# One TensorE semaphore increment per unit and bank, in a spectral and feed-forward kernel on one core

## The chip, the core and the metric

The kernel runs on one core of a Trainium2 chip. The core has a matmul engine (TensorE; PE in the profile, with its weight loads listed apart as PEld), VectorE (DVE), ScalarE (ACT), GpSimd (POOL), a queue engine that issues most transfers (SyncE; SP), and 16 DMA engines. Each engine runs its own list of instructions in order. They wait for each other through semaphores: an instruction can add to a counter when it is done, and an instruction of another engine can wait until that counter has reached a number.

The metric is the device time of one execution in microseconds (us). For the kernel before it is 258.02 us, the median of three runs (257.98 to 258.78).

## The reference

Four steps follow each other on a matrix of 2048 rows (S) by 448 columns (D), in bf16. Two of them (A) are a two-dimensional Fourier filter of the normalised input, two (B) are a feed-forward layer with a squared ReLU. Both A steps use the same filter, both B steps the same weights.

```python
def _A_ref(x, w_r, w_i):
    X = rfft2(x.astype(float32))              # over rows and columns
    y = irfft2(X * (w_r + 1j * w_i), s=(S, D)).astype(bfloat16)
    return y
def _B_ref(x, w1, b1, w2, b2):
    h = einsum("bsd,df->bsf", x, w1) + b1     # 448 -> 1792
    h = where(h > 0, h, 0); h = h * h
    return einsum("bsf,fd->bsd", h, w2) + b2  # 1792 -> 448
x = A_x
x = x + _A_ref(_layernorm(x), A_w_r, A_w_i)
x = x + _B_ref(_layernorm(x), B_w1, B_b1, B_w2, B_b2)
x = x + _A_ref(_layernorm(x), A_w_r, A_w_i)
x = x + _B_ref(_layernorm(x), B_w1, B_b1, B_w2, B_b2)
```

## The kernel before

The Fourier transforms are matmuls with constant matrices, in stages. Stage A1 (first layer) or A2 (second) transforms part of the rows into `XA`; stage TD transforms the columns, into `U` (the buffer is `arena`); stage B goes on with the rows, into `EF` (also `arena`); stage W multiplies by the filter on VectorE, into `T3` (the buffer is `wide`); stage Bi is the first half of the way back along the rows, into `VT`; stages TI and AI undo the rest, into `wide` and `x_sb`. The feed-forward layer follows: normalised rows are transposed by DMA (L708) or by matmuls with `J_sb` into `wide`, `h_part` and `h_pairs` make the hidden layer in `arena`, and `o_tile` multiplies it by the second weights and adds to `x_sb`. In the first feed-forward layer, `fold` and two additions per tile of rows (L775, `wide<-xin`) and `second_A` already begin the second Fourier layer.

All results of matmuls go to PSUM, a memory of eight banks. ScalarE or VectorE copies them out (L746 on ACT, L747 on DVE, both from `evac`); then the bank can be used again.

The kernel is written through a recorder. Each operation is added to `_Sched` with what it reads and writes, and `add` finds the operations that it depends on (`op.deps`): the last writer of what it reads, and the last writer and all the readers of what it overwrites. So an operation on VectorE that overwrites a buffer read by sixteen matmuls depends on all sixteen. Matmuls are gathered in units, runs of matmuls that are issued one behind the other; a matmul knows the PSUM tile that it adds to (`d.tile`), and a copy knows the tiles that it takes out (`op.takes`). The order of the units on each engine is written out by hand in `ORDER`.

`schedule` ends with a loop that marks each operation that anybody depends on (`has_dep`). `assign_tickets` numbers the marked operations of an engine 1, 2, 3 and so on. `emit` writes the instructions out: a marked operation increments its engine's semaphore by one when it is done, and an operation that depends on others waits for the highest of their numbers on each engine, unless its engine has waited for as high a number already. A dependency between two matmuls needs no wait, except in `h_pairs`, where matmuls on the two halves of the array add to one tile and one half waits for the other.

Stage Bi matters below. One of its units has 32 matmuls: two streams of 16, one on the upper and one on the lower 64 rows of the array, interleaved so that two matmuls run beside each other. Its stationary operand is a piece of `T3` (`wide`), its moving operand a piece of `H_sb` (128 columns). Each layer has eight such units:

```python
u = sch.new_unit("pe", 64, "row")
m = _Tile(2) if v in MERGE else None
...
if m:
    evac(V.rearrange("p t q c -> p q t c"), m[...], EV["Bi"])
else:
    for q in range(2):
        evac(V[:, :, q], t[q][...], EV["Bi"])
```

For the five units v in `MERGE` one copy takes both streams (1,024 columns); for the other three there are two copies of 512 columns, and each waits for the last matmul of its stream. The unit issued last, in either layer, is of the second kind. Stage TI begins when all eight units have been copied to `VT`. In the gaps of its plan the kernel issues matmuls on a tile of ones (L1361), whose results nobody uses. All other matmuls are recorded by one helper, `mm`, and bear its line, L721.

Of the kernel before, what the change touches and what calls it, by code (L numbers as in the profile page):

```python
# [291 lines left out]
class _Sched:  # L292
# [83 lines left out]
    def schedule(self):  # L376
# [100 lines left out]
        while total:  # L477
# [26 lines left out]
            start, u, e = choice[0][0], choice[1], choice[2]  # L504
            if e == "pe":

                while self.warm_fn is not None:
# [15 lines left out]
                    d = _Op("pe", self.warm_fn(bk[1], n), False, unit, 195.0)  # L523
# [56 lines left out]
        self.done = done  # L580
        for e in self.ENGINES:
            for op in self.ops[e]:
                for d in op.deps:
                    d.has_dep = True

# [867 lines left out]
```

## Time and profile before

| | before |
|---|---|
| median of three runs | 258.02 us |
| the profiled execution | 258.13 us |
| its span, first to last instruction | 256.3 us |
| PE busy | 247.0 us, 2,462 matmuls |
| DVE busy | 193.3 us |
| ACT busy | 167.2 us |
| granted TensorE clock | 1.00 throughout |
| matmuls of stage Bi (`ps<-H_sb,wide`) | 512, in 29.1 to 38.3 us and 147.0 to 156.5 us |

Times in views of the trace count from the first instruction of the program. In a timeline row stand the start, the length from the first to the last of the instructions taken together, the engine, the line, the operation, the buffers (`out<-in`), the shapes, the number of instructions, and in square brackets the idle time of the engine just before and who ended it. "issue" stands where the profile shows nothing that was waited for. The chain of work that ended last goes from the last instruction back, at each step to what released it; its rows give start, length, engine, buffer and line.

### The profile page before, as it was taken

The numbers are of one execution on the slowest core, as the hardware profiler recorded it, in microseconds if no ns is written. First come the engines' busy times: TensorE is split into PE (matmuls) and PEld (weight loads), VectorE is DVE, ScalarE is ACT, GpSimd is POOL, SyncE is SP. The second block draws the span as 40 slices with busy tenths as digits, with TensorE's granted clock in tenths as the row PEclk, the third lists the DMA queues.
The fourth block names the chain that finished last, engine by engine and source line by source line (L and its number), as shares of the span: only waits on it lengthen the run. The fifth ranks groups of instructions, "written<-read, shape, count | busy, mean of one in ns | idle before, by whom it ended". The sixth has DMA issues, their size and how long they took to land.

```text
span 256.3 us, 6151 instructions
## 1 busy us (share of the span) xinstructions
PE 247.0 (96%) x2462; PEld 154.4 (60%) x2462; DVE 193.3 (75%) x628; ACT 167.2 (65%) x362; POOL 12.5 (5%) x26
## 2 busy tenths in 40 slices
PE   7899988999999999999999998999999999999996
PEld 2578677886544555554567677898544445544454
DVE  3994988889872899997999997999993079320543
ACT  5896988995287894016847997999459784006600
POOL 3870000000000000000000000000000000000000
PEclk9999999999999999999999999999999999999999
DMA  6999944121111000130000000021134001152004
GB/s 196 372 329 372 290 142 145 33 48 36 48 41 43 0 4 0 41 42 3 0 3 1 3 3 3 3 41 45 42 79 41 0 3 24 39 92 72 3 0 145
DMA packets 24080, 18.10 MB, mean 71 GB/s; under 512 B 16082, under 2 KB 22706, under 8 KB 24052
## 3 DMA queue, kind: packets, MB, share of 16 engines
q1 hardware_dynamic: 22756, 13.22, 19.8%
q0 software_dynamic: 576, 3.69, 4.1%
q10 hardware_dynamic: 720, 0.80, 0.9%
q8 instruction: 19, 0.31, 0.5%
q14 instruction: 9, 0.07, 0.1%
HBM read 12.20 MB, written 1.84 MB: 55 GB/s over the span
## 4 chain that ended last, share of the span: by engine, by line
PE 82%; DMA 7%; ACT 4%; DVE 3%; issue 1%; POOL 1%; SPq 0%; DVEq 0%; POOLq 0%
PE ps L721 81%; DMA Wt<-in_A_w_r_dram,ix 4%; ACT arena L746 2%; DMA FA_sb<-c_FA 2%; DMA wide<-wide 2%; ACT wide L746 1%; DVE wide L775 1%; ACT VT L746 1%; DVE x_sb L1214 1%; PE ps L1361 0%; POOL Wt L824 0%; DVE arena L747 0%; POOL Fs L758 0%; DVE st L851 0%; SPq L713 0%
## 5 line engine op out<-in xcount | busy, mean ns | idle before, releaser
L721 PE MATMUL ps<-wide,W_sb 64*128 64x512 bf16 (+1 forms) x770 | 90.0, 346 | 0.1
L721 PE MATMUL ps<-W_sb,arena 128*128 128x448 bf16 (+3 forms) x476 | 86.8, 342 | 0.0
L721 PEld LDWEIGHTS ps<-wide,W_sb 64*128 64x128 bf16 (+1 forms) x770 | 51.4, 95 | 36.1 <-DMA wide<-wide 0.9
L740 ACT ACTIVATE arena<-ps,b1col 128x512 bf16<-128x512 f32 x84 | 51.9, 691 | 29.1 <-PE ps L721 28.8
L721 PEld LDWEIGHTS ps<-W_sb,arena 128*128 128x128 bf16 x476 | 45.6, 98 | 38.1 <-ACT arena L740 0.4
L775 DVE TENSOR_TENSOR arena<-arena 128x512 bf16<-128x512 bf16 (+1 forms) x140 | 44.0, 362 | 29.7 <-ACT arena L740 29.7
L1092 ACT ACTIVATE VT<-x_sb 128x448 bf16<-128x448 bf16 x28 | 16.1, 582 | 13.2 <-DVE x_sb L1068 13.2
L746 ACT ACTIVATE arena<-ps 128x896 bf16<-128x896 f32 (+1 forms) x27 | 20.6, 839 | 3.3 <-PE ps L721 3.3
L740 ACT ACTIVATE mv<-mv,epst 128x1 f32<-128x1 f32 (+1 forms) x45 | 12.8, 297 | 11.9 <-DVE mv L852 11.6
L775 DVE TENSOR_TENSOR wide<-arena,Wt 128x896 bf16<-128x896 bf16 x32 | 17.7, 619 | 1.2 <-DMA Wt<-in_A_w_r_dram,ix 1.2
L740 ACT ACTIVATE arena<-ps 128x256 bf16<-128x256 f32 x56 | 17.9, 400 | 0.9 <-PE ps L721 0.7
L746 ACT ACTIVATE XA<-ps 128x512 bf16<-128x512 f32 (+1 forms) x28 | 15.3, 596 | 3.3 <-PE ps L721 3.3
L721 PE MATMUL ps<-H_sb,wide 64*128 64x128 bf16 x512 | 16.0, 216 | 0.9 <-issue 0.6
L1214 DVE SCALAR_TENSOR_TENSOR x_sb<-ps,mv,xin 128x448 bf16<-128x448 f32 (+2 forms) x13 | 8.0, 643 | 11.7 <-PE ps L721 11.5
L721 PEld LDWEIGHTS ps<-H_sb,wide 64*128 64x128 bf16 x512 | 14.4, 94 | 3.3 <-issue 1.6
L721 PE MATMUL ps<-wide,VT 64*128 64x512 bf16 x42 | 15.8, 376 | 0.0
L746 ACT ACTIVATE wide<-ps 128x896 bf16<-128x896 f32 (+3 forms) x20 | 14.1, 762 | 2.2 <-DVE wide L747 1.1
L746 ACT ACTIVATE VT<-ps 128x512 bf16<-128x512 f32 (+1 forms) x16 | 12.6, 822 | 1.7 <-PE ps L721 1.4
L1361 PE MATMUL ps<-ones 128*128 128x512 bf16 (+2 forms) x32 | 10.1, 437 | 2.8 <-ACT VT L746 1.1
L757 ACT ACTIVATE wide<-x_sb,rstd 128x448 bf16<-128x448 bf16 x12 | 7.8, 665 | 6.3 <-DVE mv L784 6.0
L747 DVE CAST arena<-ps 128x448 bf16<-128x448 f32 (+1 forms) x11 | 8.8, 831 | 3.2 <-PE ps L721 3.2
L1068 DVE SCALAR_TENSOR_TENSOR x_sb<-ps,mv,xin 128x448 bf16<-128x448 f32 x16 | 10.3, 676 | 0.8 <-PE ps L721 0.7
(79 smaller groups left out, 274.7 us busy)
## 6 DMA issues: line engine op xcount, KB each, us to landing
out_dram<-x_sb SPq DMA_DIRECT2D x15, 112.0 KB, 1.8
W_sb<-in_B_w_dram SPq DMA_DIRECT2D x1, 1568.0 KB, 7.8
H_sb<-c_H SPq DMA_DIRECT2D x2, 768.0 KB, 10.9
W_sb<-in_B_w_dram SPq DMA_DIRECT2D x1, 1344.0 KB, 11.7
xin<-in_A_x_dram SPq DMA_DIRECT2D x3, 224.0 KB, 4.8
G_sb<-c_G SPq DMA_DIRECT2D x1, 512.0 KB, 6.0
xin<-in_A_x_dram ACTq DMA_DIRECT2D x2, 224.0 KB, 4.6
VT<-in_B_w_dram SPq DMA_DIRECT2D x2, 192.0 KB, 3.2
```

The source lines that it names most:

```text
L721: return sch.add("pe", lambda e: e.matmul(_res(o), lhsT, rhs, start=start, stop=stop, skip_group_check=skip), [lhsT, rhs], [o], cost=cost, ...
L740: sch.add("act", lambda e: e.activation(o, _res(i), func, **kw), rd, [o], cost=c)
L746: op = sch.add(engs[0], lambda e: e.activation(o, _res(i), ACT.Copy) if h[0].eng == "act" else e.tensor_copy(o, _res(i)), [i], [o], cost=c ...
L747: e.tensor_copy(o, _res(i)), [i], [o], cost=c[engs[0]], unit=unit)
L757: op = sch.add(engs[0], lambda e: e.activation(o, i, ACT.Copy, scale=s) if h[0].eng == "act" else e.tensor_scalar(o, i, s, 1.0, op0=ALU.mu ...
L775: sch.add(eng, lambda e: e.tensor_tensor(o, _res(a), b, op), [a, b], [o], cost=_free(o) / rate + 69.0)
L1068: small(lambda e, xx=xx, xi=xi, r=r, m=m: e.scalar_tensor_tensor(out=xx, in0=_res(r), scalar=m, in1=xi, op0=ALU.subtract, op1=ALU.add), [r ...
L1092: op = sch.add("act", lambda e, i=i, o=o, x=x, h=h: e.activation(o, x, ACT.Square, accum_out=sd[:, i, 1:2]) if h[0].eng == "act" else e.sc ...
L1214: small(lambda e: e.scalar_tensor_tensor(out=o, in0=_res(i), scalar=rs[0] if rs else 1.0, in1=xi, op0=ALU.add if t >= 4 and last else ALU. ...
L1361: return lambda e: e.matmul(ps[:, b, 0:n], ones[:], ones[:, None, :].to_broadcast([P, n // P, P]), start=True, stop=True)
```

## The change

Three lines are added to the loop at the end of `schedule`:

```diff
         for e in self.ENGINES:
             for op in self.ops[e]:
+                if e != "pe":
+                    op.deps = [d.unit.ops[-1] if d.eng == "pe" and d.unit is not None and d.tile not in op.takes else d
+                               for d in op.deps]
                 for d in op.deps:
                     d.has_dep = True
```

An operation of another engine that depends on a matmul because it overwrites what the matmul reads now depends on the last matmul of that matmul's unit instead. An operation that copies the matmul's tile out of PSUM keeps its dependency on the last matmul of that tile. So matmuls in the middle of a unit are no longer marked, unless a tile ends with them or another half of the array waits for them, and only marked ones increment the semaphore. In the built programs 1,937 of the 2,462 matmuls increment the semaphore before, and 401 after; of the 512 matmuls of stage Bi all 512 before, and 22 after.

The order of instructions on every engine stays as it is, and so do their operands. The numbers that others wait for change, since there are fewer marked matmuls. Ten waits name another matmul than before: two on DVE (L775, `wide<-xin`), eight on SP (six transposes and two transfers into `VT`); two of the eight fall away, since SP has waited for as much already. All lines behind the change have numbers higher by three.

## Prediction

> **What bounds the kernel now.** I read the page first: the shares of busy time, then the chain that ended last, by engine.
>
> ```profile
> span 256.3 us, 6151 instructions
> PE 247.0 (96%) x2462; PEld 154.4 (60%) x2462; DVE 193.3 (75%) x628; ACT 167.2 (65%) x362; POOL 12.5 (5%) x26
> PE 82%; DMA 7%; ACT 4%; DVE 3%; issue 1%; POOL 1%; SPq 0%; DVEq 0%; POOLq 0%
> ```
>
> TensorE carries the chain for 82% of the span. An edit that changes no matmul can gain in two ways: the matmuls come closer together, or one of the short stretches shrinks in which the chain leaves PE. The chain in order of time shows where those are (start, length, who):
>
> ```profile
> 33.40 0.38 issue
> 33.78 3.75 PE ps L721 x127
> ...
> 37.78 0.99 PE ps L721 x13
> 38.77 0.69 DVE VT L747
> 39.46 0.14 issue
> 39.60 5.66 PE ps L721 x74
> ...
> 45.29 90.69 PE ps L721 x699
> ...
> 153.60 3.59 PE ps L721 x96
> 157.19 0.59 ACT VT L746
> ...
> 157.83 0.39 PE ps L1361
> ...
> 163.66 58.14 PE ps L721 x461
> ...
> 253.99 0.03 issue
> 254.01 0.33 DVE x_sb L1214
> ```
>
> Two things are to be seen. From 45.29 to 135.98 and from 163.66 to 221.80 PE runs without leaving the chain, so whatever comes earlier ahead of these stretches ends the kernel earlier by as much. And the chain leaves PE behind stage Bi of both layers: at 38.77 for a copy into `VT` on DVE, at 157.19 for one on ACT. TI cannot start before these copies.
>
> **Do the increments slow the matmuls?** Stage Bi is the densest place. Two stretches of its matmuls alone (length; busy and count of PE, then of PEld; clock, DMA), and their group on the page (busy us, mean ns):
>
> ```profile
> 33.78:37.31 3.53, 3.53 (x127) 3.53 (x128) 1.00 0.48 111
> 153.60:156.46 2.86, 2.86 (x96) 2.68 (x96) 1.00 0.02 6
> ...
> L721 PE MATMUL ps<-H_sb,wide 64*128 64x128 bf16 x512 | 16.0, 216 | 0.9 <-issue 0.6
> ```
>
> 3.53 us by 126 steps is 28.0 ns a matmul. In the second row the last matmul's own 0.216 us (the mean in the group's row) comes off: 2.64 by 95 is 27.8 ns. At the full clock and without a gap, all of these matmuls increment the semaphore. So increments do not hold PE back, and I cost the matmuls' own pace at **nothing gained**.
>
> **Do they delay those who wait?** These are the copies of stage Bi in the first layer, and the end of its matmuls:
>
> ```profile
> 34.42 1.02 ACT L746 ACTIVATE VT<-ps 128x1024 bf16<-128x1024 f32 x1
> 35.51 0.60 ACT L746 ACTIVATE VT<-ps 128x512 bf16<-128x512 f32 x1
> 36.01 1.02 ACT L746 ACTIVATE VT<-ps 128x1024 bf16<-128x1024 f32 x1
> 37.70 1.02 ACT L746 ACTIVATE VT<-ps 128x1024 bf16<-128x1024 f32 x1 [0.68 <-PE ps L721]
> 37.78 0.55 PE L721 MATMUL ps<-H_sb,wide 64*128 64x128 bf16 x13 [0.25 <-issue]
> 38.76 0.69 DVE L747 CAST VT<-ps 128x512 bf16<-128x512 f32 x1 [0.92 <-PE ps L721]
> ```
>
> The copies at 34.42, 35.51 and 37.70 belong to the units issued fourth, fifth and seventh, and each waits for the last matmul of its unit. One unit (32 increments) lies between the first two, two (64) between the latter: 1.09/32 = 34.1 ns and 2.19/64 = 34.2 ns. PE issues a matmul every 28.0 ns, so the copies keep step with something slower than the matmuls, and fall behind by 32 x 6.1 = 0.2 us a unit. The lag is there to be seen: PE's last matmul ends at 37.78 + 0.55 = 38.33, while the copies start at 38.76. For a plain distance take the last two rows of the chain: from the end of the last matmul to the addition it is 0.03. So I read the semaphore as taking one increment of TensorE every 34 ns, with a queue behind it that empties only where PE pauses.
>
> The Trainium skill, "TensorE: Matmul & The Clock Gate", section "The cost: per-tile semaphore tail", says that increments on every matmul serialise and states 26.3 ns for each in the tail. The serialising agrees with the rows above; the figure doesn't, since 26.3 is less than the 28.0 ns between matmuls, and by it no queue would form here and the sum below would be nil.
>
> **The sum, first layer.** Of a unit's 32 increments one or two stay, so nothing queues. The last copy on DVE then starts at 38.33 + 0.03, about 38.36 instead of 38.76. That is 0.40 us earlier; its matmul is the last but one, which ends some 0.03 before 38.33, so I take **0.42**. The copy on ACT beside it goes as early, because the one ahead of it (37.70) waited 0.68 itself. Earlier in the layer another wait shrinks:
>
> ```profile
> 31.53 1.09 ACT L746 ACTIVATE VT<-ps 128x512 bf16<-128x512 f32 x2 [0.34 <-PE ps L721]
> 32.66 0.39 PEld L721 LDWEIGHTS ps<-H_sb,wide 64*128 64x128 bf16 x14 [0.23 <-ACT VT L746]
> ```
>
> ACT's copies at 31.53 would start up to 0.34 earlier, and PE's wait of 0.23 at 32.66 would go. But at 33.40 PE stops again until 33.78, in the "issue" of the chain, and once more at 37.78, 127 matmuls on. No engine ends those stops in the profile, they come after equal numbers of instructions, so I read them as the supply of instructions. An earlier arrival waits longer there: I cost it at **0**, and at 0.22 if the stop moves along.
>
> **The sum, second layer.**
>
> ```profile
> 149.29 0.96 ACT L746 ACTIVATE arena<-ps 128x896 bf16<-128x896 f32 x1
> 150.33 1.02 ACT L746 ACTIVATE VT<-ps 128x1024 bf16<-128x1024 f32 x1
> 150.33:153.46 3.13, 3.13 (x5) 1.00 0.00 0
> 153.57 2.71 PEld L721 LDWEIGHTS ps<-H_sb,wide 64*128 64x128 bf16 x96 [0.27 <-issue]
> 156.12 1.02 ACT L746 ACTIVATE VT<-ps 128x1024 bf16<-128x1024 f32 x1 [0.34 <-PE ps L721]
> 157.18 0.60 ACT L746 ACTIVATE VT<-ps 128x512 bf16<-128x512 f32 x1
> 157.22 0.69 DVE L747 CAST VT<-ps 128x512 bf16<-128x512 f32 x1 [0.75 <-PE ps L721]
> ```
>
> Instructions of ACT that wait for nothing overlap by about 0.10 (35.51 + 0.60 = 36.11, next start 36.01). The copy at 150.33 starts 0.08 behind the end of the one before (150.25), so without the queue it starts 0.17 earlier. ACT is then busy without a gap up to 153.46 (third row), and 0.11 later PE loads weights again: **0.17** reaches PE. At the end, the copy of 156.12 comes 0.34 of idle time and the 0.10 of overlap earlier: ready by 155.56 + 0.04 (32 matmuls of 28 ns ahead of 156.46), ACT free for it at 155.68. It starts at 155.68 and ends at 156.70; the last one starts at 156.60 to 156.64 and ends at 157.24 where it ended at 157.78. That is **0.54**. DVE's copy loses its 0.72 (157.22 against 156.46 + 0.04), so ACT's is the one that stays latest. PE then meets TI 0.54 earlier, with the 0.17 together 0.71.
>
> **Moved waits.** SP's transposes start at 49.0 and later (first row), over ten us behind the matmuls of Bi that they name, and the transfers into `VT` stand behind transposes in SP's queue; nothing. On DVE the tighter of the two:
>
> ```profile
> L708 SPq DMA_TRANSPOSE wide<-x_sb x2: 1233/1285/1337, 49.0 to 168.2; - x2
> ...
> 124.83 1.07 PE L721 MATMUL ps<-Fs,wide 128*128 128x128 bf16 x16
> 125.73 0.66 DVE L775 TENSOR_TENSOR wide<-xin 128x224 bf16<-128x224 bf16 x3
> ```
>
> Even the last of the sixteen ends at 125.90, so the addition could start at most 0.2 later; behind it on DVE wait two more additions and the squares of the hidden layer. PE alone carries the chain here (the 90.69 row): 0, and -0.2 if that cover is gone.
>
> Sum: 0.42 + 0.71 = **1.13 us**, from 258.13 to **257.0**. The execution profiled lies 0.11 above the median, within the spread of the three runs, and I don't correct for it. The ends for the terms: 0.42 + 0.54 - 0.2 = 0.76 below, 0.42 + 0.22 + 0.71 = 1.35 above.
>
> **The rivals.**
>
> *The supply of instructions takes part of it.* PE stopped at 33.78 and 37.78, 4.0 us apart, with 127 matmuls between. If 4.0 us is the least for so many, then in the second layer, where PE would now pass its units faster, a stop of up to 4.0 - 127 x 0.028 = 0.4 comes up that its wait of 0.27 covers today. Against it: 96 matmuls run there without any stop (the 153.60 row). Gain 1.13 - 0.4 or less: 257.4 to 257.7. Chance 0.14.
>
> *The queue exists only while a profile is taken*, or increments are not what the copies wait for. Then the time stays at 258.0. For it: only a profiled execution shows the rows. Against it: that execution took 258.13, and executions that are not recorded, with 1.1 us less waiting, would have to lie near 257.0, not at 258.02. Chance 0.10. The 26.3 ns of the Trainium skill's section on the semaphore tail ("TensorE: Matmul & The Clock Gate") would lead here.
>
> *Slower, by a transfer.* PE waits for a transpose once in the last layer, and starts anew at 227.17:
>
> ```profile
> DMA to landing us min/median/max: 2.7/2.8/4.1
> 223.01 4.11 DMA wide<-wide
> 227.17 26.81 PE ps L721 x196
> ```
>
> This one took 4.11, the longest of twelve. All that happens beside it shifts with the change. If it lands after more than 4.11 + 1.13 = 5.2 us, the kernel is slower than before; by 0.8 (258.8) at 6.0. For it: its length is already out of line. Against it: what it meets comes from the same chain and shifts alike. Chance 0.05.
>
> *More than the sum*: the stop at 33.78 moves too, or copies that start earlier free banks that I hold for free already. 256.4 to 256.7. Chance 0.05.
>
> **How the numbers follow.** My forecast has 0.66: 257.0, by the terms' ends 256.8 to 257.4. The range takes in the rival of supply, the larger gain, and half of the case of no change: 256.4 to 258.0. A measurement of this kernel can tell about 0.3% (0.77 us, below 257.25) from no change. Faster: 0.66 less 0.04 for its upper end, and the 0.05: 0.67. Slower 0.05. Within 0.3%: the rest, 0.28.
>
> **What would show it.** Right: the copies of Bi start 0.04 behind the last matmul of their unit, DVE's idle times of 0.92 and 0.75 before its last copies shrink by 0.4 and 0.7, Bi's matmuls keep 28 ns, and TI begins 0.4 earlier in the first layer and 1.1 earlier in the second. Wrong: copies that still lag by 0.2 us a unit (the queue is none of increments), matmuls that come closer than 28 ns (they held PE back after all), a gain in the first layer that has gone by 45.29 (another engine is late there), or new stops of "issue" inside Bi.

## The result, and the profile after

The changed kernel takes 257.30 us (median of 20 runs) where the kernel before, on the same chip, takes 258.78 (20 runs). The ratio is 0.9939, with a 95% interval of 0.9920 to 0.9957: a gain of 1.58 us, between 1.1 and 2.1. Runs in a slower state are left out of the ratios: two of the changed kernel's 20 (259.53 and 260.27 us; the other 18 have a median of 257.20), and among the experiments below two runs of the kernel before, of 427.65 and 516.20 us. The forecast was 1.13 us, at the lower end of the interval. A second measurement of the changed kernel (e8 below) gave 0.9939 again.

The profiled execution took 256.61 us. Its page, part 1, and the chain's shares by engine:

```profile
span 254.8 us, 6150 instructions
PE 246.0 (97%) x2462; PEld 153.9 (60%) x2462; DVE 193.3 (76%) x628; ACT 166.5 (65%) x362; POOL 12.5 (5%) x26
PE 82%; ACT 7%; DVE 4%; DMA 2%; issue 1%; POOL 1%; SPq 0%; DVEq 0%; POOLq 0%
```

The engines do the same work. The chain of work that ended last, in order of time (start, length, who), with the places that the prediction showed:

```profile
32.72 1.35 issue
34.07 4.13 PE ps L724 x140
38.20 0.69 DVE VT L750
38.89 0.14 issue
39.02 5.66 PE ps L724 x74
44.69 0.03 issue
44.72 90.12 PE ps L724 x689
...
155.76 0.68 ACT VT L749
156.43 0.05 issue
156.48 0.39 PE ps L1364
156.87 1.57 PE ps L724 x24
...
162.31 90.16 PE ps L724 x685
252.47 0.02 issue
252.50 0.33 DVE x_sb L1217
```

The copies of stage Bi and the matmuls ahead of them, from the timeline of the changed kernel:

```profile
34.07 4.08 PE L724 MATMUL ps<-H_sb,wide 64*128 64x128 bf16 x140 [1.35 <-issue]
37.30 1.02 ACT L749 ACTIVATE VT<-ps 128x1024 bf16<-128x1024 f32 x1 [0.25 <-PE ps L724]
38.19 0.69 DVE L750 CAST VT<-ps 128x512 bf16<-128x512 f32 x1 [0.32 <-PE ps L724]
...
150.94 4.76 PE L724 MATMUL ps<-H_sb,wide 64*128 64x128 bf16 x160
155.80 0.68 DVE L750 CAST VT<-ps 128x512 bf16<-128x512 f32 x1
```

In the first layer the last matmul of Bi ends at 34.07 + 4.08 = 38.15, and DVE's copy starts 0.04 later; it was 0.43. In the second the matmuls end at 155.70 and the copy starts 0.10 later; it was 0.76. The matmuls' pace is as before: (4.08 - 0.22)/139 is 27.8 ns.

The difference of the two profiled spans, 1.5 us, can be laid out along PE:

| stretch on PE | before | after | change |
|---|---|---|---|
| span's start to the end of the first stop, first layer | 33.78 | 34.07 | +0.29 |
| from there to the last matmul of Bi | 4.55 | 4.08 | -0.47 |
| from there to the first matmul of TI | 1.27 | 0.87 | -0.40 |
| from there to the last 160 matmuls of Bi, second layer | 111.92 | 111.92 | 0.00 |
| these 160 matmuls | 4.94 | 4.76 | -0.18 |
| from their end to TI after the L1361/L1364 matmul | 1.76 | 1.17 | -0.59 |
| from there to the last addition | 95.79 | 95.63 | -0.16 |

(The 111.92 is from 39.60 to 151.52 before, from 39.02 to 150.94 after.) The first row is a matter of the first stop "issue", which ended later in this execution; the experiments return to it. The second row is the second stop of the execution before (at 37.52, 0.25 on the chain), which did not come in this one. It belongs with the third row: before, the last copy followed the increments and not the matmuls, as e4 below shows, so the second stop cost nothing there. Together the two rows are 0.87 us in the first layer, and the fifth and sixth are 0.77 in the second. The last row is PE's wait for a transpose, which ended at 227.17 before: the wait is no longer on the chain, and the longest transpose took 3.8 instead of 4.1.

### The profile page after: what moved, and what is told of

The parts are those of the page before. It is cut to its first block, busy times and chain, and to the rows that moved or that the text cites. A ratio compares the mean times of both kernels' runs of the same rounds, so it can differ in the third digit from the quotient of the medians.

```text
span 254.8 us, 6150 instructions
## 1 busy us (share of the span) xinstructions
PE 246.0 (97%) x2462; PEld 153.9 (60%) x2462; DVE 193.3 (76%) x628; ACT 166.5 (65%) x362; POOL 12.5 (5%) x26
## 4 chain that ended last, share of the span: by engine, by line
PE 82%; ACT 7%; DVE 4%; DMA 2%; issue 1%; POOL 1%; SPq 0%; DVEq 0%; POOLq 0%
PE ps L724 82%; ACT arena L749 4%; ACT VT L749 2%; DMA FA_sb<-c_FA 2%; ACT wide L749 1%; DVE st L854 1%; DVE Fs L761 1%; DVE XA L750 1%; PE ps L1364 0%; POOL Wt L827 0%; DVE x_sb L1217 0%; POOL Fs L761 0%; SPq L716 0%; POOL VT L750 0%; DVE VT L750 0%
## 5 line engine op out<-in xcount | busy, mean ns | idle before, releaser
L1364 PE MATMUL ps<-ones 128*128 128x512 bf16 (+2 forms) x32 | 9.6, 420 | 2.6 <-DVE mv L855 1.0
```

Of the source, the lines that this page charges most:

```text
L1364: return lambda e: e.matmul(ps[:, b, 0:n], ones[:], ones[:, None, :].to_broadcast([P, n // P, P]), start=True, stop=True)
```

## Experiments

Ten runs were made in three groups (e1 to e4, e5 to e8, e9 and e10); e8 is the changed kernel once more, and e10 is the kernel of e6. Each group had its own runs of the kernel before on the same chip, with medians of 258.50, 258.88 and 258.98 us. The ratios are those on record, and some differ from the quotient of the two medians by up to 0.4% (e7: 0.9887 against 0.9923), so differences of that size between runs are not to be read from one of the two alone.

| run | us, median (runs) | ratio to before | 95% interval |
|---|---|---|---|
| e1: Bi alone | 256.18 (6) | 0.9915 | 0.9890 to 0.9940 |
| e2: all but Bi | 258.61 (12) | 1.0008 | 0.9988 to 1.0027 |
| e3: Bi's increments back | 258.56 (12) | 0.9991 | 0.9970 to 1.0013 |
| e4: on another semaphore | 258.76 (12) | 0.9999 | 0.9980 to 1.0019 |
| e5: every second matmul | 257.89 (9) | 0.9935 | 0.9906 to 0.9964 |
| e6: changed, weights later | 256.05 (6) | 0.9861 | 0.9828 to 0.9893 |
| e7: changed, 36 matmuls more | 256.89 (6) | 0.9887 | 0.9850 to 0.9923 |
| e8: changed again | 257.36 (12) | 0.9939 | 0.9909 to 0.9968 |
| e9: before, weights later | 257.40 (12) | 0.9961 | 0.9934 to 0.9988 |
| e10: e6 again | 256.04 (6) | 0.9898 | 0.9867 to 0.9929 |

### Where the gain is made: e1 and e2

```diff
-... d.tile not in op.takes else d
+... d.tile not in op.takes and d.unit.tag[:2] == "Bi" else d      # e1
+... d.tile not in op.takes and d.unit.tag[:2] != "Bi" else d      # e2
```

> The change for matmuls of stage Bi alone: their 490 unneeded increments go, the 1,046 others of the change stay. Theory of the queue (34 ns for each increment, which only Bi's 28 ns a matmul outruns): as the changed kernel, about 1.5 us under the kernel before; the last copies into VT start 0.03 to 0.1 us behind Bi's last matmul in both layers. Rival, that the number of increments counts wherever they stand: 490 of 1,536, about a third of the gain, 0.5 us.

> The change for all matmuls but those of stage Bi: 1,046 increments go, Bi keeps its 512. Theory of the queue: as the kernel before, within 0.3 us (stage B loses its lag of 0.1 us, which nothing on the chain waits for); the last copies into VT start 0.4 us behind Bi's last matmul in the first layer and 0.75 in the second. Rival, that the number of increments counts wherever they stand: two thirds of the gain, 1.0 us under the kernel before.

Of the 1,536 increments that the change takes away, Bi's 490 are the gain, and the other 1,046 are worth nothing that these runs can measure. (e1 lies below e8, but their intervals overlap.) The timeline of e2, first layer:

```profile
32.83 5.17 PE L724 MATMUL ps<-H_sb,wide 64*128 64x128 bf16 x164
38.83 0.69 DVE L750 CAST VT<-ps 128x512 bf16<-128x512 f32 x1 [0.71 <-PE ps L724]
```

The matmuls end at 38.00 and the copy starts 0.83 later. I had expected 0.4, as in the execution of the kernel before. In e2 PE does not stop a second time in Bi, so the matmuls end earlier; the copy, which follows the queue, does not start earlier by it. This is the first sign of what the forecast had too small.

### Increments or waits: e3

```diff
+        for op in self.ops["pe"]:
+            if op.unit is not None and op.unit.tag[:2] == "Bi":
+                op.has_dep = True
```

> The changed kernel with all its changed waits, but each matmul of Bi increments TensorE's semaphore again, though nobody waits for the 490 numbers added. Theory of the queue: the gain is gone, within 0.3 us of the kernel before, with lags of 0.4 and 0.75 us behind Bi's last matmul. Rival, that the gain comes from the waits that moved or fell away: as the changed kernel, 1.5 us under the kernel before, lags under 0.1 us.

All waits are those of the changed kernel, and the gain is gone. The ten moved waits have no part in it that can be measured. The timeline, both layers:

```profile
32.83 4.50 PE L727 MATMUL ps<-H_sb,wide 64*128 64x128 bf16 x142
38.16 0.69 DVE L753 CAST VT<-ps 128x512 bf16<-128x512 f32 x1 [0.92 <-PE ps L727]
...
152.99 2.86 PE L727 MATMUL ps<-H_sb,wide 64*128 64x128 bf16 x96
156.60 0.69 DVE L753 CAST VT<-ps 128x512 bf16<-128x512 f32 x1 [0.75 <-PE ps L727]
```

The lags are 0.83 (37.33 to 38.16) and 0.75 (155.85 to 156.60).

### Whose queue it is: e4

```diff
                 elif op.has_dep:
                     ins.then_inc(sem[(ename, False)], 1)
+                elif ename == "pe" and op.unit is not None and op.unit.tag[:2] == "Bi":
+                    ins.then_inc(spare, 1)
```

> The changed kernel, but the 490 matmuls of Bi that increment nothing there increment a second semaphore that nobody waits for. If the queue stands at TensorE, one for all its increments: the same lags as before the change, 0.4 and 0.75 us, and a time within 0.3 us of the kernel before. If it stands at the semaphore, each with its own: lags under 0.1 us, and the time of the changed kernel, 1.5 us under the kernel before.

```profile
35.11 4.15 PE L725 MATMUL ps<-H_sb,wide 64*128 64x128 bf16 x140 [1.46 <-issue]
40.09 0.69 DVE L751 CAST VT<-ps 128x512 bf16<-128x512 f32 x1 [0.92 <-PE ps L725]
...
154.93 2.86 PE L725 MATMUL ps<-H_sb,wide 64*128 64x128 bf16 x96
158.55 0.69 DVE L751 CAST VT<-ps 128x512 bf16<-128x512 f32 x1 [0.74 <-PE ps L725]
```

The increments that go to the spare counter hold up those of the other one: the lags are 0.83 and 0.76, and nothing is gained. So there is one queue for both counters. This run also gives the price afresh. PE has stood for 1.46 us, so the queue is empty when 140 matmuls begin at 35.11. The copy waits for the 139th. The first increment comes 0.23 (the length of a matmul that follows a pause) after 35.11; 138 more at 34.1 ns take 4.71; with the plain distance of 0.03 that is 40.08. The copy started at 40.09. In the kernel before it started as long behind the end of the first stop: 38.76 - 33.78 = 4.98 us, as 40.09 - 35.11 here, though the one execution had a second stop and the other had none.

The traces also hold the time of each increment. Here are those of TensorE behind the first stop of Bi in the first layer, and in its last 160 matmuls in the second (e5 is the next run):

```
                        first    last   increments  from one to the next
before, first layer     34.02   38.77   140         34 or 35 ns, mean 34.2
before, second layer   151.76  157.19   160         34 or 35 ns, mean 34.2
e4, both counters       35.35   40.10   133 + 7     34 or 35 ns, mean 34.2
e5, second layer       154.95  158.15    60         55 or 56 ns, but around the ends of units
```

In the kernel before the second stop leaves no gap: the queue held increments all through it. In e4 the two counters take turns in one row of increments. And 11 increments by ACT and DVE fall into the first stretch without a gap in TensorE's, so they do not stand in this queue. In none of the twelve traces are two increments of TensorE less than 34 ns apart.

### The spacing from which it queues: e5

```diff
+            if op.unit is not None and op.unit.tag[:2] == "Bi" and op.unit.ops.index(op) % 2 == 0:
+                op.has_dep = True
```

> The changed kernel, but the first matmul of each pair in Bi increments the semaphore too: 272 of 512, one per 56 ns. Theory of a queue that takes one increment in 34 ns: it keeps up, the last copies start under 0.12 us behind Bi's last matmul in both layers, and the time is that of the changed kernel. Rival, that each increment adds its own delay at any spacing: half the lag of before, 0.2 to 0.4 us in each layer, and half the gain lost, 0.7 us.

The ratio is near that of e8, and the lags are gone: 0.03 and 0.10. The second layer is the test, for in the first the matmuls of the profiled execution were further apart (the last section says why). Its rows:

```profile
154.83 3.29 PE L727 MATMUL ps<-H_sb,wide 64*128 64x128 bf16 x108
158.22 0.69 DVE L753 CAST VT<-ps 128x512 bf16<-128x512 f32 x1
```

272 increments at one per 56 ns cost nothing; 512 at one per 28 ns cost the whole gain. It is the spacing that counts; the step lies between 28 and 56 ns, and the increments themselves, 34 ns apart, say where.

### The stop of PE: e6 to e10

In the changed kernel PE stood still for 1.35 us inside Bi, longer than before (0.38 on the chain), and the runs scatter by more than the gain (255.58 to 260.27 us). The prediction had read the stop as the supply of instructions. e6 holds back a load, e7 shifts the count of instructions, e8 is the changed kernel as it is.

```diff
+        w = [op for op in self.ops["dve"] if op.unit.tag[:3] == "W0."]                            # e6, e9, e10
+        next(op for op in self.ops["sp"] if op.unit.tag[:7] == "L.W1_sb").deps.append(w[11])
...
+                    if n == 512 and len(self.ops["pe"]) <= 45:                                   # e7
+                        d.fn = self.warm_fn(bk[1], 128)
+                        self.ops["pe"] += [_Op("pe", d.fn, False, unit / 4, 195.0) for _ in range(3)]
```

> The changed kernel, but the loads of the first feed-forward weights (1.5 MB, issued at 22 us) wait for a multiplication of stage W, which ends at about 34 us; SP's loads behind them wait too. If the stop of PE in the first layer's Bi (no releaser in the profile; up to 1.6 us in the runs so far) comes from instructions that load late beside heavy traffic, it goes, and the time is 0.5 to 1 us under the changed kernel. If PE's own progress sets when those instructions load, the stop stays, and the time is the same within 0.3 us. If the weights land too late for the matmuls at 44 us, it is slower.

> The changed kernel, but each of the first 12 matmuls on ones (512 columns) is issued as four of 128: 36 matmuls more ahead of Bi, 72 instructions with their weight loads, for the same time. If the stop in the first layer's Bi is the supply of instructions in blocks, it stands at the same place in the count, which is 36 matmuls earlier in Bi: behind its 88th instead of its 124th. If it waits for data or for another engine, it stays behind the 124th. The time should stay that of the changed kernel within 0.5 us, since the stop's length varies.

> The changed kernel once more, as it is, beside the three others. Theory of the queue: 1.5 us under the kernel before (1.1 to 2.1), lags under 0.12 us. If the stop in the first layer's Bi is another length than 1.35 us, the time of the profiled execution moves with it.

The timelines of e7 and of e8, from the start of Bi:

```profile
28.68 1.96 PE L727 MATMUL ps<-H_sb,wide 64*128 64x128 bf16 x64
30.57 0.57 PE L727 MATMUL ps<-arena,G_sb 64*64 64x448 bf16 x8
31.09 0.62 PE L727 MATMUL ps<-H_sb,wide 64*128 64x128 bf16 x16
31.99 5.40 PE L727 MATMUL ps<-H_sb,wide 64*128 64x128 bf16 x176 [0.28 <-issue]
```

```profile
29.56 1.96 PE L724 MATMUL ps<-H_sb,wide 64*128 64x128 bf16 x64
31.45 0.57 PE L724 MATMUL ps<-arena,G_sb 64*64 64x448 bf16 x8
31.96 1.63 PE L724 MATMUL ps<-H_sb,wide 64*128 64x128 bf16 x52
34.31 3.75 PE L724 MATMUL ps<-H_sb,wide 64*128 64x128 bf16 x127 [0.72 <-issue]
38.31 0.55 PE L724 MATMUL ps<-H_sb,wide 64*128 64x128 bf16 x13 [0.25 <-issue]
38.85 0.69 DVE L750 CAST VT<-ps 128x512 bf16<-128x512 f32 x1 [0.75 <-PE ps L724]
```

With stage B's eight between, the stop stands behind 64 + 8 + 52 = 124 matmuls in e8, and behind 64 + 8 + 16 = 88 in e7: 36 earlier, for 36 matmuls put in ahead. It keeps its place in the count of instructions, not in the work. (In time, e7 and e8 have overlapping intervals.) e8 also shows the second stop, 127 matmuls on; its last copy starts 38.85 - 34.31 = 4.54 us behind the end of the first stop, where that of the changed kernel's first profile starts 38.19 - 34.07 = 4.12 behind.

The trace lists transfers of instructions in blocks of 16 KB. I take them for TensorE's: there are 19 for its 4,924 instructions, which is 259 each, close to the 254 between the two stops. The end of the one ahead of the stop, and the start of PE's next matmul, in us:

```
                         before after  e1    e3    e4    e5    e8  | e6    e9    e10
block has arrived         32.26 32.61 32.02 31.72 33.68 33.30 32.77 | 30.00 29.80 29.99
PE goes on                33.78 34.07 33.46 33.18 35.11 34.86 34.31 | 33.24 32.42 32.80
difference                 1.52  1.46  1.44  1.46  1.43  1.56  1.54 | no stop
```

In seven executions PE goes on 1.43 to 1.56 us after the block has arrived. e7, with its stop at another place, gives 1.44 (30.55 and 31.99), and the second stops give 1.43 (before: 36.35 and 37.78), 1.51 (e7: 34.33 and 35.84) and 1.58 (e8: 36.73 and 38.31). (In e2 the block was there at 32.06, but PE came to the place only at 33.73, and hardly stopped.) In the three with the weights held back the block is there by 30.00, and PE does not stop. So the loads held back, the first 1.5 MB of weights and what SP issues behind them, are what makes the block late; the stretch from 24 to 30 us in the changed kernel and in e6 (length; PE, PEld, DVE, ACT, POOL; clock, DMA's share, GB/s):

```profile
24.00:30.00 6.00, 6.00 (x122) 4.57 (x113) 5.57 (x10) 6.00 (x10) 0.00 (x0) 1.00 1.05 341
```

```profile
24.00:30.00 6.00, 5.34 (x94) 3.90 (x88) 4.69 (x8) 5.76 (x9) 0.00 (x0) 1.00 0.53 164
```

The DMA engines are full in the one and half used in the other. e6 took 1.31 us less than e8 (medians), more than the 0.5 to 1 that I had expected. e6 and e10, the same kernel, have the lowest medians, though e1's is only 0.13 us above. e6's six runs lie within 1.04 us (255.45 to 256.49) and e10's six within 1.71, where e8's twelve spread over 3.03; but e9's twelve, weights held back as well, spread over 3.53, so that the scatter comes from the stop is not shown.

e9 and e10 ask whether the two edits add:

> The kernel before, all its increments kept, with the loads of the first feed-forward weights held back as in the run e6. If the queue of increments and the stop of PE are two causes, the stop goes here too (about 1 us), the lags behind Bi's last matmul stay (0.8 us in both layers, since no stop lets the queue run empty), and the time is about 1.2 us under the kernel before and about 1.5 us over the run with both edits. If the lag was only hidden by the stop or made by it, the two edits do not add: under 0.5 us between this run and the one with both.

> The changed kernel with the loads of the weights held back, once more, beside the kernel before with the same loads held back. Two causes that add: 2.5 to 3 us under the kernel before, lags under 0.3 us, no stop in the first layer's Bi.

The end of Bi in the first layer, in e9 and in e10; no stop in either:

```profile
30.73 5.98 PE L723 MATMUL ps<-H_sb,wide 64*128 64x128 bf16 x192
37.54 0.69 DVE L749 CAST VT<-ps 128x512 bf16<-128x512 f32 x1 [0.79 <-PE ps L723]
38.38 0.35 PE L723 MATMUL ps<-TI_sb,VT 112*128 112x224 bf16 x2 [1.13 <-DVE VT L749]
```

```profile
31.34 5.73 PE L726 MATMUL ps<-H_sb,wide 64*128 64x128 bf16 x192
37.33 0.68 DVE L752 CAST VT<-ps 128x512 bf16<-128x512 f32 x1
38.15 0.54 PE L726 MATMUL ps<-TI_sb,VT 112*128 112x224 bf16 x4 [0.55 <-DVE VT L752]
```

They add, as far as these runs can tell. Holding the loads back is worth 0.4% with the increments kept (e9; 0.6% by the medians). From e9 to e10 the medians differ by 1.36 us, about as the changed kernel differs from the one before. In these rows the first layer gives 0.84 us of it: from the last 192 matmuls of Bi to TI it takes 38.38 - 30.73 = 7.65 in e9, and 38.15 - 31.34 = 6.81 in e10. Of that, 0.25 is in the matmuls themselves (5.98 and 5.73), the rest behind them. e10's lag of 0.26 is no queue: its DVE was still at the copy before.

## Why the prediction was right, and which term was too small

- **Increments do not slow the matmuls.** Right: 27.8 ns a matmul with and without them.
- **One increment per 34 ns, and a queue.** Right. The increments themselves come 34.2 ns apart; e4 started a stretch with an empty queue, and the sum came within 0.01 us of its last copy; e5 shows that one per 56 ns leaves no queue. The 26.3 ns that the Trainium skill states ("TensorE: Matmul & The Clock Gate", section "The cost: per-tile semaphore tail") does not hold here: by it e3 would have been as fast as the changed kernel, and it was as slow as the one before.
- **Second layer, 0.71 us.** Right: 0.59 behind Bi's end and 0.18 in the last 160 matmuls, 0.77.
- **First layer, 0.42 us.** This is the term that was mis-sized. The prediction held the end of Bi's last matmul at 38.33 and let the copy come down to it. But 38.33 has PE's second stop in it, in which no matmul started from 37.31 to 37.78. Before the change that stop was hidden: the copy started 4.98 us behind the end of the first stop, with a second stop (before) or without (e4), since it followed the queue of increments. When the queue is gone the copy follows the matmuls, 4.12 us behind the first stop without a second one (after) and 4.54 with one (e8). So the layer is worth 0.86 us without the second stop in the changed kernel, and 0.44 with it. The forecast had the second case without saying so. Of the seven profiled executions without the queue (after, e1, e5, e6, e7, e8, e10) e8 had this stop at full length, and e7 one of 0.10 us; how many of the timed runs had it is not known. With the second layer's 0.77 it is 1.63 or 1.21 us; the 1.58 measured is nearer to the first, but the interval, 1.1 to 2.1, holds both.
- **The time, 257.0 us.** That the median of 257.30 lies so near is in part luck: over 20 runs the kernel before took 258.78, 0.65 more than the 258.13 from which the forecast started, and the gain was 0.45 larger.
- **The 0.22 that the stop would swallow.** Right in kind. PE came to the stop 0.68 us earlier (32.72 against 33.40), but 0.54 of it was there when Bi began (28.60 against 29.14); it went on 0.29 later all the same. The stop follows the arrival of a block of instructions, and nothing that Bi saved moved it.
- **Moved waits, 0.** Right (e3).
- **The rivals.** The time did not stay as it was, and e1, e2 and e3 part by Bi's increments alone. Whether the queue also forms when nothing is recorded is not shown: a span and a granted clock are on record for each run of the changed kernel and of the experiments, so all of them may have been recorded. No new stop came up in the second layer. The longest transpose landed after 3.8 us, not later than before.

## What to carry to other kernels

Increment a semaphore only where somebody waits for it, and look first where matmuls run beside each other on parts of the array: there they can end faster than the engine's increments are taken (here one per 28 ns against 34), and the lag shows at the copy behind the last of them, not on TensorE. A recorder that depends on every reader of a buffer marks far too many; the last one of an in-order run is enough. When an engine stands still and the profile names nobody, count instructions between the stops, and look at what the DMA engines carry at that time.

## What the runs showed of the hardware that was not expected

- TensorE's increments come no closer than 34 ns in any of the twelve traces, and those of two counters stand in one queue (e4).
- A short stop of an engine can be free while its increments queue: the second stop in Bi left no gap among them in the kernel before, and cost 0.42 us in e8 (4.54 against 4.12).
- A block of instructions that arrives late stopped TensorE for up to 2.07 us, and PE went on some 1.5 us after the arrival; holding back the first weights, and the loads behind them, was worth 1.31 us with the change (e6 against e8, medians).
- After the longest stop, in e5, the granted clock fell. The windows of the stop, of the matmuls behind it and of the stretch after these (the clock stands ahead of DMA's share):

```profile
32.79:34.86 2.07, 0.00 (x1) 0.01 (x2) 2.04 (x4) 0.94 (x2) 0.00 (x0) 1.00 0.11 35
34.86:38.00 3.14, 3.14 (x66) 3.14 (x68) 0.87 (x2) 1.86 (x3) 0.00 (x0) 0.56 0.50 111
38.00:40.60 2.60, 2.60 (x81) 2.50 (x77) 1.58 (x2) 1.54 (x2) 0.00 (x0) 0.88 1.05 349
```

66 matmuls took 3.14 us there, 48 ns each. In e4, after 1.46 us of standing, the clock stayed at 1.00. One execution does not show that the stop lowered the clock. But the clock missing in the windows above comes to 1.7 us (0.44 of 3.14 and 0.12 of 2.60), a mean of 0.993 over the span of 257.5 us, and this mean is on record for 3 of the changed kernel's 20 runs (258.20, 259.53 and 260.27 us), for 2 of e5's 9 and 1 of e8's 12, and for none of the 24 runs with the weights held back (e6, e9, e10).
